# Moving eight 128x1024 integer additions from VectorE to GpSimd in a fused attention and rational-FFN kernel

## The chip, the cores and the metric

The kernel runs on one core of a Trainium2 chip. The metric is the device time of one execution in microseconds (us), from a run without a profile; lower is better. Three such runs of the kernel before gave 809.83, 808.62 and 809.86 us, with a median of 809.83. A profile is one further execution that is traced. Engines: PE is TensorE (matrix products), DVE is VectorE, ACT is ScalarE, POOL is GpSimd, SP is SyncE, whose queue issues the transfers between HBM and the on-chip memory.

## The reference

There are two parts. The first is a two-step attention for 8 batches and 8 heads with 576 tokens of 64 features: 32 packed queries `p` attend over `k` and `v`, and then the 576 queries `q` attend over the 32 packed rows. The second is a feed-forward layer on the 4608 tokens with 512 features, whose activation is a ratio of two polynomials.

```python
def sm_attn(qq, kk, vv):
    s = scale * np.matmul(qq, kk.transpose(0, 1, 3, 2))
    s = s - np.max(s, axis=-1, keepdims=True)
    a = np.exp(s)
    a = a / (np.sum(a, axis=-1, keepdims=True) + 1e-09)
    return np.matmul(a, vv)
p_packed = sm_attn(p, k, v)
out = sm_attn(q, p_packed, p_packed)
...
h = x @ w_in
h2 = h * h
h3 = h2 * h
P = a[0] + a[1] * h + a[2] * h2 + a[3] * h3
Q = 1.0 + np.abs(b[0]) * np.abs(h) + np.abs(b[1]) * h2
g = P / (Q + 1e-06)
return (g @ w_out).astype(np.float32)
```

The inputs come in as float64. `w_in` is 512x2048, `w_out` is 2048x512.

## The kernel before, in words

**Units.** The feed-forward work is cut into 128 units: 8 batches, two halves of 288 tokens, and 8 chunks `c` of 256 hidden features. For a unit, PE makes `h` from the attention weights (tiles `AH`, `AL`: a high and a low part of each number) and from a chunk matrix `m`; ACT and DVE make the ratio (`Y`, `U`, `V`), ACT and POOL split the result in a high and a low part (`gh`, `gl`), and PE multiplies these by the split `w_out` (tiles `w`) into `acc`. The chunk matrix `m` of a batch is made by `m_chunk` (L731): PE multiplies the batch's packed rows by chunk `c` of the converted `w_in` (tile `win`), and ACT splits the product. So the first eight units of the first batch need the chunks `c` = 0 to 7 of `win` one after the other, and nothing of `m` can be made for a chunk before its conversion is over. Later batches find `win` ready.

**Conversion of the float64 weights.** `convert` (L389) turns one pair of blocks of float64 words into float32. The raw words are loaded by SP into buffers that are free for the time being (`m0` to `m3` first, then buffers of the `w` ring). A pair of `w_in`'s words is one chunk `c`: 128x1024 numbers. Its steps are: ACT scales the high halves `hi` in place (L406) and brings the upper bits of the low halves `lo` into `di` (L408), which for `w_in` is the chunk's own place in `win`; DVE takes the sign (L409), shifts `hi` by three bits and puts the sign in (L410), and adds `di` to it as 32-bit integers (L411). In the trace and in the order this addition appears as `CUSTOM_DVE_ANT_0` or `ISA` with 128x2048 uint16. For `w_in` the sum is the finished chunk. For `w_out` it is split in two parts on ACT and POOL (L416). There are 8 such pairs of `w_in`, 7 pairs of `w_out`, and two single blocks of `w_out`.

**What sets the order.** All operations are recorded, not issued, and then put in order by `Planner` (L33): it gives each a cost by engine and columns, schedules them several times over the five engines by their dependences, and keeps the order of the best of its schedules. Each engine then runs its list strictly in order. So moving a recorded operation to another engine, at another cost, makes the planner work out a new order for every engine. The planner's costs know nothing of two engines that hold each other up. Because all operations are issued in one place, the profile gives them all the line L216, and groups have to be told apart by tiles.

**Names.** `kx` holds the keys, the queries and the scores of a batch's attention, `small` its maxima and sums, `pn` its packed queries, `nat` loaded blocks of `k`, `q`, `v`. For the first batch DVE subtracts the maxima and multiplies by the reciprocal sums in `kx` and makes `AL` (`eng` in L510); for the later ones POOL does. `G` collects the columns that the main products leave out. In the order's names the first number counts tiles: `m_1_82`, `m_2_83`, `m_3_115`, `m_4_116`, `w_3_117`, `w_4_118`, `w_6_120` and `w_8_132` are the raw words of the chunks 0 to 7 of `w_in`; `w_5_119` and `w_7_121` are the first raw pairs of `w_out`, and `w_11_158` is the first split pair.

Of the kernel before, what the change touches and what calls it, by code (L numbers as in the profile page):

```python
# [15 lines left out]
I32 = mybir.dt.int32  # L16
# [231 lines left out]
def attention_rational_ffn(  # L248
# [35 lines left out]
    nc = Planner(tc.nc)  # L284
# [75 lines left out]
    def load_words(n):  # L360
        while len(words_in) < min(len(words), converted + n):
            r = len(words_in)
            kind, i, n2 = words[r]
            used = [x for x, _ in words_in]
            free = [x for x, end in room if r < end and x not in used[converted:]]
            free = [x for x in free if x[0] is not w_ring or x[1] < NCH - 2 or started]
            if not free and r == converted and n2 == 1:
                free = [(o_ring, 0)]
            if not free:
                return  # L370
            x = min(free, key=lambda x: max((j for j in range(r) if used[j] == x), default=-1))
            raw = x[0].at(x[1], [P, n2 * 512], I64)
            if kind == "in":
                c = i // 2
                for y in range(2):
                    src = w_in[2 * y * P : (2 * y + 2) * P, c * CF : (c + 1) * CF].rearrange("(x p) f -> p x f", p=P)
                    nc.sync.dma_start(raw[:, 512 * y : 512 * (y + 1)].rearrange("p (x y) -> p x y", x=2), src)
            else:
                for y in range(n2):
                    nc.sync.dma_start(raw[:, 512 * y : 512 * (y + 1)], w_out[(i + y) * P : (i + y + 1) * P, :])  # L380
            words_in.append((x, raw))
# [3 lines left out]
    def split(x, hi, lo, eng=nc.gpsimd):  # L385
        nc.scalar.copy(hi, x)
        eng.tensor_sub(lo, x, hi.bitcast(F32))

    def convert():  # L389
        nonlocal converted  # L390
        if converted == len(words):
            return
        load_words(AHEAD)
        (kind, i, n), raw = words[converted], words_in[converted][1]
        x = 4 if kind == "in" else n
        w = raw.bitcast(I32).rearrange("p (x y two) -> p x y two", x=x, two=2)
        lo, hi = w[:, :, :, 0], w[:, :, :, 1]

        if kind == "in":
            dst = win[:, i // 2]  # L400
            di = dst.bitcast(I32)
        else:
            dst = lo.bitcast(F32)
            di = w_ring.at(i // 2, [P, n * DM], I32) if n == 2 else full_ring.next(dtype=I32)
            di = di.rearrange("p (x y) -> p x y", x=n)
        nc.scalar.activation(hi.bitcast(F32), hi.bitcast(F32), AF.Copy, scale=REBIAS)  # L406

        nc.scalar.activation(di, lo.bitcast(U32), AF.Copy, scale=2.0**-29)  # L408
        nc.vector.tensor_scalar(lo, hi, -0x80000000, None, ALU.bitwise_and)  # L409
        nc.vector.scalar_tensor_tensor(hi, hi, 3, lo, ALU.logical_shift_left, ALU.bitwise_or)  # L410
        nc.vector.tensor_add(dst.bitcast(I32), hi, di)  # L411
        if kind == "out":
            if i // 2 not in W:
                W[i // 2] = w_ring.at(i // 2)
            for y in range(n):
                split(dst[:, y, :], *(W[i // 2][:, (i + y) % 2, x, :] for x in range(2)))  # L416
        converted += 1
        load_words(AHEAD)
# [454 lines left out]
    for _ in range(PRE):  # L873
        convert()
# [30 lines left out]
    for u in range(NU + LAG + 2):  # L905
        if u < NU:
            pipe[u] = hidden(*units[u])
        stage(u)
        if 0 <= u - LAG < NU:
            acc_block(u - LAG, 0)  # L910
        filler(2 * u)
        stage(u)
        stage(u - 2)
        stage(u - 1)
        for x in rem.get(u, ()):
            remainder(*x)
        convert()
        while converted < len(words) and due(words[converted]) <= u + 1:
            convert()
        if 0 <= u - LAG < NU:  # L920
            acc_block(u - LAG, 1)
        filler(2 * u + 1)
# [30 lines left out]
```

## Time and profile before

| | |
|---|---|
| median of three runs | 809.83 us |
| the profiled execution | 808.45 us |
| its span, first to last instruction | 806.7 us |
| mean granted TensorE clock | 0.958 |
| busy PE, DVE, ACT, POOL | 745.5, 709.1, 666.0, 463.9 us |
| instructions on PE, DVE, ACT, POOL | 5416, 1310, 1482, 462 |

Of the profiled execution's 808.45 us, 1.75 lie outside the span. The page cuts the span in 40 slices of 20.2 us; a view by stages gives each engine's busy time in stretches that one chooses; a view by groups gives the count, the busy time and the mean of all instructions of one shape; a timeline lists the instructions of an engine with their start and duration. In a timeline an instruction's duration overlaps the next one's start by a little, so that the place that it takes in its engine's time is the distance between two starts.

### The profile page before, as it was taken

How to read it: one execution, taken by the hardware profiler on the slowest of the kernel's cores; microseconds unless marked ns; L12 is line 12 of the kernel's file. 1: busy time of each engine (PE TensorE's matmuls, PEld its weight loads, DVE VectorE, ACT ScalarE, POOL GpSimd, SP SyncE). 2: the span in 40 equal slices, each digit the busy share in tenths (PEclk: the TensorE clock that was granted, in tenths of full speed). 3: DMA queues.
4: the chain of work that ended last, by engine and by line, in shares of the span. 5: the costliest groups of instructions: out<-in, count | busy, mean ns of one | idle time of the engine just before them, and what ended most of it. 6: DMA issues, size and time to landing. Idle time of an engine off the chain costs nothing.

```text
span 806.7 us, 15198 instructions
## 1 busy us (share of the span) xinstructions
PE 745.5 (92%) x5416; PEld 585.4 (73%) x5416; DVE 709.1 (88%) x1310; ACT 666.0 (83%) x1482; POOL 463.9 (58%) x462
## 2 busy tenths in 40 slices
PE   6376686899999999999999999999999999999997
PEld 4154464578877788768878788678877887778886
DVE  2988999898899788998899789998899789998873
ACT  4788797799888798889888798889888788998972
POOL 0003564675568455766578555756568456766663
PEclk9765799799999999999999999999999999999999
DMA  8993238202550206220730209120820214000001
GB/s 267 280 298 110 105 78 110 43 5 79 67 86 1 79 18 96 56 57 28 94 58 1 82 15 119 33 56 27 103 49 5 75 33 67 1 2 27 27 1 39
DMA packets 168876, 56.04 MB, mean 69 GB/s; under 512 B 140384, under 2 KB 158048, under 8 KB 168800
## 3 DMA queue, kind: packets, MB, share of 16 engines
q1 hardware_dynamic: 168800, 55.07, 31.4%
q8 instruction: 42, 0.69, 0.4%
q14 instruction: 34, 0.28, 0.1%
HBM read 45.62 MB, written 9.44 MB: 68 GB/s over the span
## 4 chain that ended last, share of the span: by engine, by line
PE 70%; DVE 10%; ACT 8%; SPq 4%; DMA 4%; issue 2%; POOL 1%; DVEq 0%; POOLq 0%
PE acc L216 35%; PE h L216 22%; PE at L216 13%; DVE Y L216 5%; SPq L216 4%; ACT Y L216 2%; DVE w L216 1%; ACT U L216 1%; ACT V L216 1%; ACT w L216 1%; DMA w<-in_q_dram 1%; ACT sq L216 1%; DVE V L216 1%; POOL w L216 1%; DVE kx L216 1%
## 5 line engine op out<-in xcount | busy, mean ns | idle before, releaser
L216 PE MATMUL acc<-w,gh 128*128 128x512 f32 x1024 | 330.5, 405 | 19.3 <-ACT w L216 15.0
L216 PEld LDWEIGHTS acc<-w,gh 128*128 128x128 f32 x1024 | 186.7, 191 | 72.7 <-ACT w L216 16.6
L216 POOL TENSOR_TENSOR U<-U,sq 128x576 f32<-128x576 f32 x118 | 168.9, 1432 | 75.4 <-ACT U L216 43.3
L216 PE MATMUL h<-AH,m 128*128 128x288 f32 x1024 | 192.0, 309 | 8.8 <-DVE Y L216 6.1
L216 POOL TENSOR_TENSOR gl<-Y,gh 128x512 fp32r<-128x512 f32 x128 | 167.7, 1310 | 50.5 <-ACT gh L216 23.3
L216 PE MATMUL acc<-w,gl 128*128 128x512 f32 x512 | 193.2, 398 | 0.3 <-POOL gl L216 0.3
L216 PEld LDWEIGHTS h<-AH,m 128*128 128x128 f32 x1024 | 162.7, 195 | 40.5 <-DVE Y L216 23.1
L216 ACT ACTIVATE Y<-h,abS 128x288 f32<-128x288 f32 x256 | 125.2, 509 | 23.5 <-PE h L216 19.3
L216 DVE TENSOR_TENSOR Y<-Y,h 128x288 f32<-128x288 f32 x256 | 109.9, 446 | 32.0 <-ACT Y L216 12.0
L216 ACT ACTIVATE sq<-h 128x288 f32<-128x288 f32 x236 | 97.5, 416 | 40.2 <-PE h L216 34.1
L216 DVE SCALAR_TENSOR_TENSOR Y<-Y,abS,h 128x288 f32<-128x288 f32 x256 | 125.5, 508 | 2.2
L216 DVE SCALAR_TENSOR_TENSOR Y<-Y,abS,V 128x576 f32<-128x576 f32 x128 | 103.4, 808 | 22.7 <-ACT V L216 22.0
L216 PEld LDWEIGHTS acc<-w,gl 128*128 128x128 f32 x512 | 96.8, 189 | 28.0 <-issue 8.5
L216 PE MATMUL h<-AL,m 128*128 128x288 f32 x512 | 113.0, 302 | 0.0
L216 POOL COPY G<-Y 128x64 f32<-128x64 f32 x128 | 35.5, 277 | 125.8 <-DVE Y L216 109.1
L216 ACT ACTIVATE U<-h 128x288 f32<-128x288 f32 x256 | 98.1, 421 | 8.7 <-PE h L216 4.3
L216 ACT ACTIVATE V<-U,one 128x576 f32<-128x576 f32 x128 | 98.0, 766 | 5.8 <-DVE Y L216 5.6
L216 DVE SCALAR_TENSOR_TENSOR Y<-V,Y 128x576 f32<-128x576 f32 x128 | 95.8, 749 | 1.8
L216 DVE SCALAR_TENSOR_TENSOR V<-U,V 128x576 f32<-128x576 f32 x128 | 96.4, 753 | 0.0
L216 ACT CAST gh<-Y 128x512 fp32r<-128x512 f32 x128 | 81.2, 634 | 7.4 <-DVE Y L216 7.0
L216 PEld LDWEIGHTS h<-AL,m 128*128 128x128 f32 x512 | 85.1, 194 | 0.9 <-issue 0.8
L216 ACT ACTIVATE V<-V 128x576 f32<-128x576 f32 x128 | 84.6, 661 | 0.6
(123 smaller groups left out, 813.2 us busy)
## 6 DMA issues: line engine op xcount, KB each, us to landing
nat<-in_k_dram SPq DMA_DIRECT2D x56, 144.0 KB, 4.1
nat<-in_q_dram SPq DMA_DIRECT2D x56, 144.0 KB, 4.2
out_dram<-o SPq DMA_DIRECT2D x15, 512.0 KB, 2.9
w<-in_moe_w_out_dram SPq DMA_DIRECT2D x14, 512.0 KB, 5.0
nat<-in_v_dram SPq DMA_DIRECT2D x28, 256.0 KB, 3.6
m<-in_moe_w_in_dram SPq DMA_DIRECT2D x8, 512.0 KB, 9.6
w<-in_moe_w_in_dram SPq DMA_DIRECT2D x8, 512.0 KB, 5.5
nat<-in_k_dram SPq DMA_DIRECT2D x2, 512.0 KB, 4.8
```

What stands on the lines that cost most here:

```text
L216: getattr(getattr(self.nc, engine), name)(*args, **kwargs)
```

## The change

The addition of `convert` goes to POOL when the words are those of `w_in`, and stays on DVE for those of `w_out`:

```diff
         nc.vector.scalar_tensor_tensor(hi, hi, 3, lo, ALU.logical_shift_left, ALU.bitwise_or)
-        nc.vector.tensor_add(dst.bitcast(I32), hi, di)
+
+        eng = nc.gpsimd if kind == "in" else nc.vector
+        eng.tensor_add(dst.bitcast(I32), hi, di)
         if kind == "out":
```

The planner makes a new order from this. The lists of all engines differ up to about a third of the kernel; DVE's is the same again from its row 432 of 1302 on, which is in the fifth half-batch.

On DVE, at the conversion of the chunks 1 and 2 in the first attention, this stood before (`ISA` is the addition):

```order
L216 SCALAR_TENSOR_TENSOR m_2_83<-m_2_83 128x1024
L216 TENSOR_REDUCE small<-kx_1_84 128x18
L216 TENSOR_TENSOR kx_1_84<-kx_1_84,small 128x576
L216 TENSOR_SCALAR small<-small 128x18
L216 ISA win<-m_2_83,win 128x2048
L216 RECIPROCAL small<-small 128x18
L216 STREAM_TRANSPOSE kx_1_84<-kx_1_84 128x576
L216 TENSOR_TENSOR kx_1_84<-kx_1_84,small 128x576
L216 SCALAR_TENSOR_TENSOR m_3_115<-m_3_115 128x1024
L216 STREAM_TRANSPOSE kx_1_84<-kx_1_84 128x576
L216 TENSOR_TENSOR AL_1_86<-kx_1_84,AH_1_85 128x576
```

and this stands there now:

```order
L216 SCALAR_TENSOR_TENSOR m_2_83<-m_2_83 128x1024
L216 TENSOR_REDUCE small<-kx_1_84 128x18
L216 TENSOR_TENSOR kx_1_84<-kx_1_84,small 128x576
L216 TENSOR_SCALAR small<-small 128x18
L216 TENSOR_SCALAR m_3_115<-m_3_115 128x1024
L216 RECIPROCAL small<-small 128x18
L216 RECIPROCAL root<-root 128x1
L216 SCALAR_TENSOR_TENSOR m_3_115<-m_3_115 128x1024
L216 TENSOR_REDUCE small<-kx_1_84 128x18
L216 TENSOR_TENSOR kx_1_84<-kx_1_84,small 128x576
L216 TENSOR_SCALAR small<-small 128x18
L216 TENSOR_SCALAR m_4_116<-m_4_116 128x1024
```

The additions are gone from the list, and the shifts of the next chunks (`SCALAR_TENSOR_TENSOR m`) stand earlier. That of chunk 1 stood behind the subtraction of the maxima in both halves of the scores and now stands ahead of the second of these (the first `TENSOR_TENSOR kx` of the rows now); that of chunk 2 stood behind both multiplications by the reciprocal sums and now stands ahead of them (the second `TENSOR_TENSOR kx` of the rows now is the first of them).

On POOL, from the packed queries of the second batch (`pn_2_107`) to the second split pair of `w_out` (`w_14_174`), this stood before:

```order
L216 COPY pn_2_107<-pn_2_107 128x2x64
L216 COPY G<-Y_2_127 128x2x32
L216 TENSOR_TENSOR gl_1_156<-Y_2_127,gh_1_155 128x512
L216 COPY pn_3_243<-pn_3_243 128x2x64
L216 TENSOR_TENSOR w_11_158<-w_5_119,w_11_158 128x512 x2
L216 COPY G<-Y_3_138 128x2x32
L216 TENSOR_TENSOR gl_2_171<-Y_3_138,gh_2_170 128x512
L216 TENSOR_TENSOR w_14_174<-w_7_121,w_14_174 128x512 x2
```

and this stands there now:

```order
L216 TENSOR_TENSOR win<-w_3_117,win 128x1024
L216 TENSOR_TENSOR win<-w_4_118,win 128x1024
L216 COPY pn_2_107<-pn_2_107 128x2x64
L216 COPY G<-Y_2_127 128x2x32
L216 TENSOR_TENSOR gl_1_156<-Y_2_127,gh_1_155 128x512
L216 COPY G<-Y_3_138 128x2x32
L216 TENSOR_TENSOR gl_2_171<-Y_3_138,gh_2_170 128x512
L216 TENSOR_TENSOR w_11_158<-w_5_119,w_11_158 128x512
L216 TENSOR_TENSOR win<-w_6_120,win 128x1024
L216 TENSOR_TENSOR w_11_158<-w_5_119,w_11_158 128x512
L216 COPY G<-Y_4_151 128x2x32
L216 COPY pn_3_243<-pn_3_243 128x2x64
```

The additions of the chunks 0 to 5 stand ahead of all other work of POOL behind its first copy; that of chunk 6 stands between the two halves of the first split pair of `w_out`, and that of chunk 7 (not shown) stands behind the second split pair.

On SP the loads of the raw words `w_3_117` now stand ahead of the four loads of `nat_3_104` instead of behind them, those of `pn_2_107` ahead of `w_6_120`, and those of `nat_6_153` behind `w_12_172` and `w_15_175`, which go into the buffers of the raw words `w_6_120` and `w_7_121`.

## The prediction

> **What bounds the kernel now.** I read the page first, for the engines' busy time over the whole and by slices.
>
> ```profile
> span 806.7 us, 15198 instructions
> PE 745.5 (92%) x5416; PEld 585.4 (73%) x5416; DVE 709.1 (88%) x1310; ACT 666.0 (83%) x1482; POOL 463.9 (58%) x462
> PE   6376686899999999999999999999999999999997
> DVE  2988999898899788998899789998899789998873
> ```
>
> PE is the busiest, but in its first eight slices of 20.2 us it is far from full, and DVE is nearly full there. The view by stages shows the change from one regime to the other (busy us of each engine, then the granted TensorE clock):
>
> ```profile
> 25.00:50.00 25.00, 11.82 (x84) 6.31 (x85) 23.59 (x40) 18.27 (x32) 0.00 (x0) 0.58 0.95 232
> 50.00:75.00 25.00, 15.48 (x110) 11.32 (x108) 21.79 (x33) 23.45 (x44) 5.73 (x6) 0.64 0.66 214
> 75.00:100.00 25.00, 18.88 (x119) 13.89 (x120) 23.28 (x36) 18.42 (x39) 13.39 (x9) 0.70 0.32 118
> 100.00:125.00 25.00, 21.73 (x175) 15.50 (x174) 24.93 (x42) 22.26 (x44) 15.15 (x13) 0.98 0.51 85
> 125.00:150.00 25.00, 16.73 (x104) 10.73 (x104) 24.88 (x45) 17.56 (x36) 15.49 (x15) 0.77 0.56 80
> 150.00:780.00 630.00, 623.48 (x4519) 498.84 (x4512) 568.29 (x1066) 541.13 (x1239) 401.73 (x403) 1.00 0.25 47
> ```
>
> From 150 us on PE is busy 623.48 of 630 us (99%): it is the bound, and no saving on DVE counts there. From 25 to 150 us DVE is busy 118.47 of 125 us (95%), and ACT leads only from 50 to 75 us (23.45 of 25). All conversions lie in this ramp. So a microsecond that the ramp gains or loses on DVE is about a microsecond at the end: the order of all engines comes back to what it was in the fifth half-batch, and PE runs through the rest.
>
> **The change part by part.** *What DVE gets rid of.* In the groups that keep shapes apart, eight additions for `w_in`, four with raw words in `m` and four in `w`, take about 1.22 us each; below them are the nearest rows of POOL.
>
> ```profile
> L216 DVE CUSTOM_DVE_ANT_0 win<-m,win 128x2048 uint16<-128x2048 uint16 x4 | 4.9, 1226 | 0.0
> L216 DVE CUSTOM_DVE_ANT_0 win<-w,win 128x2048 uint16<-128x2048 uint16 x4 | 4.9, 1216 | 0.0
> L216 POOL TENSOR_TENSOR U<-U,sq 128x576 f32<-128x576 f32 x118 | 168.9, 1432 | 75.4 <-ACT U L216 43.3 <-ACT sq L216 15.8 <-DVE Y L216 9.2
> L216 POOL TENSOR_TENSOR gl<-Y,gh 128x512 fp32r<-128x512 f32 x128 | 167.7, 1310 | 50.5 <-ACT gh L216 23.3 <-issue 15.4 <-POOL G L216 6.9
> ```
>
> The timeline of DVE in the first attention shows the place that an addition takes:
>
> ```profile
> 24.05 1.23 DVE L216 CUSTOM_DVE_ANT_0 win<-m,win 128x2048 uint16<-128x2048 uint16 x1
> 25.20 0.84 DVE L216 STREAM_TRANSPOSE kx<-at 128x288 f32<-128x288 f32 x2
> 27.34 0.72 DVE L216 TENSOR_TENSOR kx<-kx,small 128x576 f32<-128x576 f32 x1
> ...
> 31.42 1.17 DVE L216 SCALAR_TENSOR_TENSOR m<-m 128x1024 int32<-128x1024 int32 x1
> 32.49 0.75 DVE L216 TENSOR_REDUCE small<-kx 128x18 f32<-128x576 f32 x1
> 33.15 0.76 DVE L216 TENSOR_TENSOR kx<-kx,small 128x576 f32<-128x576 f32 x1
> 33.89 1.23 DVE L216 CUSTOM_DVE_ANT_0 win<-m,win 128x2048 uint16<-128x2048 uint16 x1
> 35.03 0.27 DVE L216 RECIPROCAL small<-small 128x18 f32<-128x18 f32 x1
> ...
> 37.61 0.78 DVE L216 STREAM_TRANSPOSE kx<-kx 128x576 f32<-128x576 f32 x1
> 38.30 0.73 DVE L216 TENSOR_TENSOR AL<-kx,AH 128x576 fp32r<-128x576 f32 x1
> ...
> 42.47 1.45 DVE L216 STREAM_TRANSPOSE kx<-nat 128x576 f32<-128x576 f32 x2
> 45.33 0.45 DVE L216 TENSOR_TENSOR Y<-Y,h 128x288 f32<-128x288 f32 x1 [1.41 <-ACT U L216]
> ```
>
> From 33.89 to the next start at 35.03 are 1.14 us; eight such places are 9.1 us.
>
> *What POOL gets.* No row shows an integer addition on POOL. The two rows above differ by 122 ns for 64 columns, 1.91 ns a column; 512 columns beyond the 512 make 1310 + 977 = 2287 ns. That is my estimate, 2.29 us. Bounds: half of 1310 for the low end, if integers went far faster (0.7 us), and twice 2.29 for the high end (4.6 us), if they had a slower path. I take 2.29, since it continues two rows of the same form. POOL is idle from 25 to 50 us and has 5.73 busy of 25 behind that, so its time costs nothing by itself: 8 x 2.29 = 18.3 us fit.
>
> *What DVE gets back.* The timelines of POOL and DVE show that certain instructions of the two exclude each other:
>
> ```profile
> 76.58 1.28 POOL L216 TENSOR_TENSOR gl<-Y,gh 128x512 fp32r<-128x512 f32 x1 [0.16 <-ACT gh L216]
> ...
> 87.17 3.02 POOL L216 COPY G<-Y 128x64 f32<-128x64 f32 x1
> ...
> 112.33 1.61 POOL L216 TENSOR_TENSOR gl<-Y,gh 128x512 fp32r<-128x512 f32 x1 [2.74 <-ACT gh L216]
> ```
>
> ```profile
> 77.00 1.41 DVE L216 TENSOR_SCALAR w<-w 128x1024 int32<-128x1024 int32 x1
> ...
> 87.14 0.69 DVE L216 TENSOR_SCALAR w<-w 128x1024 int32<-128x1024 int32 x1
> 87.74 2.36 DVE L216 SCALAR_TENSOR_TENSOR w<-w 128x1024 int32<-128x1024 int32 x2
> ...
> 113.43 1.60 DVE L216 SCALAR_TENSOR_TENSOR w<-w 128x1024 int32<-128x1024 int32 x1
> ```
>
> The sign operation at 77.00 took 1.41 us where the same at 87.14 took 0.69; it ended at 78.41, 0.55 after POOL's subtraction ended at 77.86. The shift at 113.43, which reads two tensors in the on-chip memory, took 1.60 instead of the 1.17 of its sister at 31.42; it ended 1.09 after POOL did at 113.94. And the copy at 87.17, a small one, took 3.02 and ended at 90.19, when two shifts of DVE had ended at 90.10. So while POOL makes an addition of 2.29 us, DVE cannot run an operation with two such inputs, nor the sign operation. The attention's `TENSOR_TENSOR kx` and `AL` have two such inputs; in before they ran while POOL was idle, so no row shows them held, and I give them what the row at 113.43 shows.
>
> Now I go down DVE's new order behind each shift that releases an addition, taking 0.1 us for the release. Chunk 0: three transposes, a maximum and a transpose come next, which nothing holds; they take 27.34 - 25.20 = 2.14, so the subtraction behind them is held 2.39 - 2.14 = 0.25. Chunk 1: a sum (33.15 - 32.49 = 0.66), then a subtraction, held 1.7. Chunk 2: the same with a multiplication, 1.7. Chunk 3: a transpose (0.69 from 37.61 to 38.30), then `AL`, held 1.7. Chunks 4 and 5: two transposes of `nat`, then operations that read `h` from the matrix products' memory, 0. Chunk 6: between 0 and 1.4, as it depends on where ACT lets the addition start; I take 0.7. Chunk 7 comes in a run of sign operations, shifts and additions of `w_out`, between 0 and 1.6: if POOL gets in first, DVE is held 1.6; if DVE's next operation always goes ahead, as in the row at 87.17, POOL waits instead and DVE loses nothing. I take 0.8. The sum is 0.25 + 3 x 1.7 + 0.7 + 0.8 = 6.85 us; its bounds are 0, if the attention's operations are not held, and about 16, if an addition takes 4.6 us (2.3 more at each of the chunks 0 to 3).
>
> On chunk 7 the Trainium skill differs from the row: by "SBUF — State Buffer", section "SBUF: two separate sides", the one of the two engines that starts first has the shared port pair for its whole instruction and the other blocks, so a waiting POOL instruction should come in between two of DVE's. The copy at 87.17 was passed over by the second shift. By the page's rule the hold for chunk 7 would be 1.6 and the sum below -1.5 us; by the row it would be 0 and the sum -3.1.
>
> *The sum.* DVE: -9.1 + 6.85 = -2.25, in round numbers -2.2 us.
>
> *What else moves.* The new order lets SP load the words of chunk 4 ahead of four blocks of `k`, and `v`'s second half behind two pairs of `w_out`.
>
> ```profile
> 19.40 10.78 SPq L216 DMA_DIRECT2D nat<-in_k_dram  x4
> 30.22 2.21 SPq L216 DMA_DIRECT2D w<-in_moe_w_in_dram  x4
> ...
> 73.17 32.11 SPq L216 DMA_DIRECT2D w<-in_moe_w_out_dram  x8
> ```
>
> ```profile
> 73.68 2.56 POOL L216 TENSOR_TENSOR w<-w,w 128x512 fp32r<-128x512 f32 x2 [2.19 <-ACT w L216]
> ```
>
> The blocks of `k` are issued half of 2.21 later, to about 31.3 us, and are first read at 42.47: covered. The pair of `w_out` at 73.17 goes into the buffer of chunk 6's raw words. It waited for DVE's addition and now waits for POOL's, which stands behind the first half of `w_11`'s split: 73.68 + 1.28 + 2.29 = 77.25, 4 us later. This pair's sign operation comes at 87.14, 14 us after its issue, so I price the delay at nothing; were the cover gone, it would cost up to about 1 us of DVE. Behind the sixth addition on POOL stand `G`, `gl` and the splits; POOL's idle time covers them. The small root computation moves to gaps: nothing.
>
> So the profiled execution's 808.45 would become 806.2, and the median of 809.83 becomes **807.6 us**. A measurement of this kernel can tell about 0.2% (1.6 us) from no change. With holds between 4 and 9 us this case gives -5 to 0 us: 804.8 to 809.8.
>
> **The rivals.** *The holds are small (full gain).* If DVE's attention operations run beside POOL, or POOL's integers are quick, DVE saves its 9.1 us. The stretch from 50 to 75 us, where ACT leads, has three of the eight additions and would keep about half of their 3.4 us, so 9.1 - 1.7 = 7.4: 802.4 us. For it speaks that no row shows a float operation of the attention held; against it, the row at 113.43.
>
> *The first attention comes late and nothing makes it up (slower).* The place is the first operation of the first unit, at 45.33, before which DVE had been idle for 1.41 us. Up to there DVE loses three additions (3.4 us), but gets holds of 0.25 + 5.1 and, by the new order, chunk 4's sign operation and shift (0.7 + 1.1) that came behind it: +3.7 on its former end at 43.92, 47.6 instead of 45.33, so 2.3 us late. In the main case DVE gets this back, because it has chunk 4's work done and no addition for the chunks 3 to 5. But from 50 to 75 us ACT is busy 94%, and its own work then starts late. If ACT stays behind until PE is the bound, the end is 2.3 us later: 812.1 us; with additions of 4.6 us the four holds would make it 9 more, which I hold for unlikely and leave out of the range. It decides when ACT reaches unit 1 more than 2 us later than now. The skill's "GPSIMD Engine Reference", section "4.1 Engine selection", would have the two-input addition left on VectorE, since GpSimd takes about twice as long; 2.29 against 1.22 us agrees with that.
>
> *Nothing changes.* ACT paces the ramp to 100 us, so that DVE's saving becomes idle time: 809.8 us. Against it stands DVE's 24.93 and 24.88 of 25 us from 100 to 150.
>
> That the change doesn't do what it says is excluded: the new lists show the eight additions on POOL.
>
> **How the numbers follow.** My forecast has 0.45 (0.33 of it beyond 1.6 us), the full gain 0.15, the slower case 0.28, no change 0.12. Faster by over 0.2%: 0.33 + 0.15 = 0.48. Within: 0.12 + 0.12 = 0.24. Slower: 0.28. The range reaches below to the full gain, and above to the slower case with somewhat longer additions: 802.0 to 813.5. Beyond its ends I leave about half of the full gain's chance below and a third of the slower one's above, 0.17.
>
> **What would show each step.** In the changed kernel's profile: the group `win` on POOL with a mean near 2.29 us; `TENSOR_TENSOR kx` and `AL` of the first attention with 2.4 instead of 0.73 us, three of them; DVE busy from 25 to 150 us less by 2 to 3 us or the same work done earlier, and the first `Y<-Y,h` near 47.6. I am wrong if these operations keep 0.73 us (then the gain is larger), if the additions take over 3 us, or if the ramp's length moves for a reason in the new order that I priced at nothing.

## The result and the profile after

The kernel with the change takes 805.23 us (median of six runs, 803.53 to 808.72), the kernel before 809.70 (six runs, 808.62 to 810.05). The ratio is 0.9947, with a 95% interval of 0.9927 to 0.9967: faster by 4.5 us, where 2.2 were forecast. The profiled execution took 803.53 us. Its page begins so (span, busy time of the engines, and the first slices of 20 us):

```profile
span 801.8 us, 15225 instructions
PE 738.4 (92%) x5416; PEld 580.3 (72%) x5416; DVE 710.1 (89%) x1302; ACT 665.6 (83%) x1482; POOL 480.1 (60%) x470
PE   6465695999999999999999999999999999999997
DVE  2999999998899789998899789998899789998883
```

Eight instructions have left DVE (1310 to 1302) and come to POOL (462 to 470). But DVE is not less busy: 710.1 us, and 709.1 before. The view by stages, with the columns of before, says where:

```profile
25.00:50.00 25.00, 11.82 (x92) 6.79 (x93) 24.69 (x34) 17.03 (x31) 9.77 (x5) 0.59 1.02 266
50.00:75.00 25.00, 15.51 (x88) 11.42 (x87) 24.05 (x38) 23.95 (x48) 13.91 (x10) 0.66 0.49 154
75.00:100.00 25.00, 16.54 (x149) 11.24 (x149) 25.00 (x34) 22.84 (x46) 15.93 (x12) 0.80 0.40 136
100.00:125.00 25.00, 20.12 (x173) 16.42 (x172) 25.00 (x43) 20.51 (x40) 12.84 (x12) 0.93 0.60 93
125.00:150.00 25.00, 18.41 (x113) 12.82 (x119) 23.95 (x43) 18.42 (x40) 12.68 (x14) 0.86 0.48 92
150.00:780.00 630.00, 623.96 (x4525) 497.73 (x4524) 569.66 (x1069) 540.91 (x1239) 403.23 (x404) 1.00 0.25 46
```

From 25 to 150 us DVE is busy 122.69 us in place of 118.47: the ramp is fuller. From 150 us on PE is busy 623.96 of 630 us, as before. ACT, which had 18.42 us of work from 75 to 100 us, has 22.84. The gain is made in this ramp: PE's busy time over the whole less that up to 150 us leaves 641.2 us of work behind 150 us, and 645.6 before. The groups that the prediction named, first on POOL, then on DVE (count, busy us and mean ns behind the bar):

```profile
L216 POOL TENSOR_TENSOR win<-w,win 128x1024 int32<-128x1024 int32 x4 | 10.0, 2511 | 9.2 <-DVE w L216 5.6 <-ACT U L216 3.7
L216 POOL TENSOR_TENSOR win<-m,win 128x1024 int32<-128x1024 int32 x4 | 9.6, 2412 | 26.7 <-DVE m L216 20.6 <-ACT m L216 3.3 <-DMA nat<-in_k_dram 2.8
```

```profile
L216 DVE TENSOR_TENSOR kx<-kx,small 128x576 f32<-128x576 f32 x4 | 6.6, 1648 | 0.0
L216 DVE TENSOR_TENSOR AL<-kx,AH 128x576 fp32r<-128x576 f32 x2 | 3.3, 1649 | 0.0
```

An addition takes 2.41 us on POOL (2.51 with one that had to wait). The means of 1648 and 1649 ns mix held and unheld operations, as the timelines of POOL and DVE show for the first attention:

```profile
22.72 2.41 POOL L216 TENSOR_TENSOR win<-m,win 128x1024 int32<-128x1024 int32 x1 [16.63 <-DVE m L216]
28.46 2.41 POOL L216 TENSOR_TENSOR win<-m,win 128x1024 int32<-128x1024 int32 x1 [3.33 <-ACT m L216]
```

```profile
25.21 0.72 DVE L216 TENSOR_TENSOR kx<-kx,small 128x576 f32<-128x576 f32 x1
...
28.91 2.59 DVE L216 TENSOR_TENSOR kx<-kx,small 128x576 f32<-128x576 f32 x1
...
34.08 2.58 DVE L216 TENSOR_TENSOR kx<-kx,small 128x576 f32<-128x576 f32 x1
...
40.53 2.55 DVE L216 TENSOR_TENSOR AL<-kx,AH 128x576 fp32r<-128x576 f32 x1
43.01 0.68 DVE L216 TENSOR_SCALAR w<-w 128x1024 int32<-128x1024 int32 x1
...
44.28 1.21 DVE L216 SCALAR_TENSOR_TENSOR w<-w 128x1024 int32<-128x1024 int32 x1
45.41 1.43 DVE L216 STREAM_TRANSPOSE kx<-nat 128x576 f32<-128x576 f32 x2
47.15 0.45 DVE L216 TENSOR_TENSOR Y<-Y,h 128x288 f32<-128x288 f32 x1 [0.31 <-ACT U L216]
```

Three operations are held, 2.55 to 2.59 us each instead of 0.72; the first of them ends at 31.50, 0.63 behind POOL's addition (28.46 + 2.41 = 30.87). The first unit starts at 47.15 instead of 45.33. All that is nearly what was forecast. What was not forecast stands at the end of the last row: DVE had waited 1.41 us for ACT's `U` there and now waits 0.31. The view of waits of DVE from 40 to 160 us (us in total, times, longest) has this in one row for before and one for after:

```profile
DVE Y L216 <- ACT U L216: 5.2, 5, 1.7
```

```profile
DVE Y L216 <- ACT U L216: 0.6, 2, 0.3
```

These waits have shrunk by 4.6 us, and the kernel by 4.5. That the two sizes agree does not yet make the one the cause of the other; the table behind the experiments sets them side by side for every kernel.

### The profile page after: what moved, and what is told of

Read it like the earlier page. It is cut to its first block, busy times and chain, and to the rows that moved or that the text cites. A ratio compares the mean times of both kernels' runs of the same rounds, so it can differ in the third digit from the quotient of the medians.

```text
span 801.8 us, 15225 instructions
## 1 busy us (share of the span) xinstructions
PE 738.4 (92%) x5416; PEld 580.3 (72%) x5416; DVE 710.1 (89%) x1302; ACT 665.6 (83%) x1482; POOL 480.1 (60%) x470
## 4 chain that ended last, share of the span: by engine, by line
PE 72%; DVE 13%; ACT 8%; DMA 3%; issue 2%; SPq 2%; POOL 0%; DVEq 0%; ACTq 0%
PE acc L216 36%; PE h L216 23%; PE at L216 13%; DVE Y L216 5%; DVE w L216 3%; SPq L216 2%; ACT Y L216 2%; ACT U L216 1%; ACT V L216 1%; DMA m<-in_moe_w_in_dram 1%; ACT sq L216 1%; DVE o L216 1%; DMA w<-in_moe_w_out_dram 1%; DMA rv<-in_v_dram 1%; DVE U L216 1%
## 5 line engine op out<-in xcount | busy, mean ns | idle before, releaser
L216 PE MATMUL h<-AH,m 128*128 128x288 f32 x1024 | 189.7, 307 | 16.0 <-DVE Y L216 12.6
L216 PEld LDWEIGHTS h<-AH,m 128*128 128x128 f32 x1024 | 160.6, 193 | 46.2 <-DVE Y L216 29.6
L216 POOL COPY G<-Y 128x64 f32<-128x64 f32 x128 | 33.7, 263 | 111.4 <-DVE Y L216 102.3
```

Of the source, the lines that this page charges most:

```text
L216: getattr(getattr(self.nc, engine), name)(*args, **kwargs)
```

## Experiments

There were two theories at first. By the forecast's, the additions that left DVE are the gain and the holds the price. By the rival, the planner's new order is the gain, and where the additions run does not matter. Each experiment was timed beside the kernel before, on the same chip, 5 to 12 times; its ratio compares the two. The chips differ between groups of experiments, so that medians of different experiments are not compared with each other to a microsecond.

**The new order, with the additions on DVE.** The planner sees the additions on POOL, and they are issued on DVE (the edit is against the changed kernel).

```diff
-            engine, calls = self.ops[i]
+            engine, calls = self.moved.get(i, self.ops[i][0]), self.ops[i][1]
...
         eng = nc.gpsimd if kind == "in" else nc.vector
         eng.tensor_add(dst.bitcast(I32), hi, di)
+        nc.moved.update({len(nc.ops) - 1: "vector"} if kind == "in" else {})
```

> The planner is told what the changed kernel tells it, so every engine's list is that of the changed kernel, but the eight additions are issued on VectorE, each at the place of the plan. First theory (the engine made the gain: 9.1 us off VectorE less about 7 of holds): without the moved additions most of the 4.5 us goes away; the new order without the move is worth about what is left over, 4.5 - 2.2 = 2.3 us, so about 807.4 us. Rival (the new order made the gain, and the engine nothing, since VectorE is as long busy as before): about 805.2 us, as the changed kernel. Second rival (an order made for GpSimd is bad with VectorE's additions in it): about 810 us or more.

Measured: 804.63 us, ratio 0.9938 (0.9925 to 0.9951). The whole gain is there with no addition moved. DVE's waits for `U` are all but gone as well:

```profile
DVE Y L216 <- ACT V L216: 1.8, 2, 1.0
DVE Y L216 <- ACT U L216: 0.4, 1, 0.4
```

The first unit starts even later than in the changed kernel:

```profile
48.34 0.77 DVE L216 STREAM_TRANSPOSE kx<-nat 128x576 f32<-128x576 f32 x1
49.03 0.42 DVE L216 TENSOR_TENSOR Y<-Y,h 128x288 f32<-128x288 f32 x1
```

It starts at 49.03, 3.7 us behind before's 45.33, with no wait in front of it, since conversion work stands where DVE used to wait. A late first unit is not a loss by itself.

**The old order, with the additions on POOL.** The reverse: planned as before, issued on GpSimd. The line in `issue` is the same as above.

```diff
         nc.vector.tensor_add(dst.bitcast(I32), hi, di)
+        nc.moved.update({len(nc.ops) - 1: "gpsimd"} if kind == "in" else {})
```

> The converse: the planner plans as before, and the eight additions go to GpSimd without a change of any other list. First theory (engine): about 2.2 us less than before, 807.5 us, with holds of about 1.7 us at the operations behind each shift that read two tensors. Rival (order): as before, 809.7 us, or slower, since GpSimd's additions take 2.4 us and hold VectorE.

Measured: 808.86 us, ratio 0.9993 (0.9981 to 1.0004). Moving the additions alone gives nothing that can be told from no change. Its waits of DVE show where the saving goes:

```profile
DVE Y L216 <- ACT U L216: 7.5, 6, 3.1
DVE w L216 <- ACT w L216: 1.2, 1, 1.2
DVE Y L216 <- ACT V L216: 0.6, 2, 0.4
```

DVE's wait for `U` grows from 5.2 to 7.5 us. Up to the end of the eleventh unit DVE is busy 127.2 us in place of 129.5, less by 2.3, and idle 26.6 us in place of 22.2: what the move saves, holds deducted, turns into waiting, and more than that. This unit ends 2.1 us later (153.8 us for 151.7), in a profiled execution that is 1.1 us longer than before's (809.59 us for 808.45).

**Shorter holds.** In the changed kernel each addition is cut in four pieces of 256 columns, so that DVE can come in between them.

```diff
-            for name, args, kwargs in calls:
+            for name, args, kwargs in self.cut(calls) if i in self.moved else calls:
...
+    def cut(self, calls):
+        (name, args, kwargs), = calls
+        return [(name, [x[:, j : j + 1] for x in args], kwargs) for j in range(4)]
```

> The changed kernel with the same lists, but each addition on GpSimd is issued as four of 256 columns. If a waiting VectorE operation gets in between two pieces, the first attention's held operations take at most 0.73 + 0.7 us instead of 2.59. First theory (the holds give back most of the saving, each microsecond of them is one at the end): about 3 us faster than the changed kernel, 802 us. Rival (VectorE's holds in the first attention are not what the end waits for, as ACT and the transfers pace it there): within 1 us of the changed kernel. Second rival (the pieces' fixed costs make the additions longer and a chunk later): slower than the changed kernel by 1 us or more.

Measured: 804.01 us, ratio 0.9932 (0.9918 to 0.9945). The first attention on DVE:

```profile
29.68 0.92 DVE L216 TENSOR_TENSOR kx<-kx,small 128x576 f32<-128x576 f32 x1
30.52 0.71 DVE L216 TENSOR_SCALAR small<-small 128x18 f32<-128x18 f32 x1
...
34.09 1.33 DVE L216 TENSOR_TENSOR kx<-kx,small 128x576 f32<-128x576 f32 x1
...
40.32 0.87 DVE L216 TENSOR_TENSOR AL<-kx,AH 128x576 fp32r<-128x576 f32 x1
...
46.53 0.41 DVE L216 TENSOR_TENSOR Y<-Y,h 128x288 f32<-128x288 f32 x1
```

The operations that were held 1.85 us each now lose 0.21, 0.62 and 0.14, but others lose some instead: the small `TENSOR_SCALAR` takes 0.71 us where it took 0.17 (at 31.42 in the changed kernel). Summed over all of DVE's operations from 22 us to the first unit, each against its free duration, 4.6 us are lost here and 5.6 in the changed kernel: the pieces spread the holds rather than remove them, the first unit starts only 0.62 us earlier, and the interval of the ratio overlaps that of the change. So this run cannot say what the holds are worth.

**Another order of the same work.** All is as in the kernel before, but the planner prices an addition of 1024 columns on DVE at 200 ns more.

```diff
-        return fixed + per * self.columns(aps[1] if name.startswith("reduce") else aps[0])
+        return fixed + per * self.columns(aps[1] if name.startswith("reduce") else aps[0]) + 200 * (name == "tensor_add" and engine == "vector" and self.columns(aps[0]) == 1024)
```

> The kernel before with all work on its old engines; only the planner's price of the eight additions on VectorE is 200 ns higher, which gives another order up to the fifth half-batch and the same behind it. Theory that the order by itself moves the time by several microseconds (the gain of the change is one such draw): a difference from before of 1.5 to 5 us, either way. Theory that orders of the same work are alike: within 1 us of 809.7.

Measured: 806.61 us, ratio 0.9962 (0.9949 to 0.9975). An order that has nothing to do with the change takes 3 us off as well, and here DVE waits 4.4 us for `U` in three waits.

**Which part of the new order.** For the next four kernels the program works out both orders and joins them; every addition stays on DVE. In the first, only SP's list of transfers is the new one; in the others all engines follow the new order for what it plans before 34, 58 or 90 us, and behind that the old one. (These are the planner's own times. On DVE its last step ahead of 58 us is chunk 6's shift, which starts at 66.78 us in the trace of that kernel, and its last step ahead of 90 us stands near 105 us of the trace.)

```diff
+        at = lambda i: (new if self.ops[i][0] == "sync" else old)[i]
```

```diff
+        first = sorted((i for i in range(len(new)) if new[i] < 34000), key=lambda i: (new[i], i))
+        done = set(first)
+        return first + sorted((i for i in range(len(old)) if i not in done), key=lambda i: (old[i], i))
```

> All eight additions on VectorE. Only SP's list of loads is the new one (the words of chunk 4 ahead of four blocks of k, the second half of v behind two pairs of w_out); the lists of the four compute engines are those of before. Theory that earlier loads make the gain: about 804.6 us, as with all lists new. Rival (the order of the compute engines makes it): 809.4 us within 1 us, or slower, if a load that comes later is missed.

Measured: 813.07 us, ratio 1.0046 (1.0033 to 1.0059), slower by 3.7 us. DVE's timeline shows where it starts:

```profile
17.65 0.16 DVE L216 SCALAR_TENSOR_TENSOR root<-ab 128x1 f32<-128x1 f32 x1 [3.83 <-DMA ab<-in_moe_b_dram]
```

The new list brings the coefficients `ab` later. In DVE's old list the small root computation stands early and waits 3.83 us for them, and the first unit then starts at 48.37 us, 3.0 later than before; the new order also puts the root's steps later, so that there is no such wait. Half of an order can be worse than either order.

> All eight additions on VectorE. The operations that the new plan puts ahead of the first product h stand first, in the new order (the first attention and the conversions of the chunks 0 to 2); all others follow in the order of before. Theory that the earlier shifts of the chunks 1 to 3 in the first attention make the gain: most of 4.8 us, so 805 to 806 us. Rival (the gain is made between the first unit and the last chunk, where ACT is busy 94% from 50 to 75 us): within 1 us of 809.4.

Measured: 809.14 us, ratio 1.0003 (0.9993 to 1.0013): no change. The first attention's new order, with the old order behind it, is not the gain.

> As the run before it, but the new order holds up to the conversion of chunk 5 and the first product of unit 3. Theory of the first attention: no better than the run before it. Theory of the stage where ACT leads: about half of the gain, 806 to 808 us.

Measured: 812.48 us, ratio 1.0035 (1.0022 to 1.0047), slower. The joint seems to cost here: DVE's two longest waits are 3.54 us for `U` at 85.77 and 2.05 for `V` at 77.54, behind the place where the lists change over.

> As the run before it, but the new order holds up to the conversion of the last chunk (7) and the products of unit 6. If the gain is made up to there, 804.6 us within 1 us; if a part of it comes from the order of what follows (the remaining words of w_out and the second attention), about 806 to 807 us.

Measured: 803.66 us, ratio 0.9924 (0.9910 to 0.9939): the whole gain, again with no addition moved. So what the new order does up to the planner's 90 us is enough, and what it does up to 58, with the old order behind it, is not. DVE's waits from 40 to 160 us:

```profile
DVE Y L216 <- ACT Y L216: 1.7, 2, 1.5
DVE Y L216 <- ACT V L216: 1.1, 2, 0.7
DVE Y L216 <- ACT U L216: 0.4, 1, 0.4
```

**One thing at a time.** In the kernel before, the stage from 60 to 85 us seemed to have three faults. DVE converted `w_out`'s first pair in turns with chunk 6; PE waited 4.91 us for this pair's copies, with the next units' `h` behind them in its list; ACT made conversions for later pairs ahead of these copies. These are the rows of PE and DVE before, and PE's waits for ACT's copies of `w` from 60 to 100 us:

```profile
73.65 1.22 PE L216 MATMUL acc<-w,gh 128*128 128x512 f32 x2 [4.91 <-ACT w L216]
69.87 1.47 DVE L216 CUSTOM_DVE_ANT_0 w<-w,w 128x2048 uint16<-128x2048 uint16 x1
PE acc L216 <- ACT w L216: 7.6, 2, 4.9
```

Each was changed alone in the old order, and then all three together. `put` gives a step (by its number) another time in the planner's old schedule, in ns, and with it another place in its engine's list.

```diff
+        put = {408: 63500.0, 409: 63600.0}
+        at = lambda i: put.get(i, old[i])
```

Steps 408 and 409 are chunk 6's sign operation and shift; the pair's addition stands at 62983.

> All eight additions stay on VectorE and the old order stays, but for one thing: on VectorE the first two steps of chunk 6's words of w_in (the shift and the combination that writes w) go behind the addition of w_out's first pair. In the kernel before, TensorE stands still for 4.91 us at 73.65 until ScalarE's copies of that pair come. Theory A (lockstep on VectorE: the pair that TensorE waits for is late because another pair is converted in the middle of it): the addition ends about 1.9 us earlier, TensorE's wait shrinks to about 3 us, and the kernel takes about 806 to 807 us. Theory B (ScalarE's list sets it: it is busy without a gap from 59.8 to 77.6 with conversions for later pairs, and the copies stand behind them): the addition comes earlier and the copies do not, 809 us. Rival C (the gain has no single place, and needs the whole new order of this stage): 809 us.

Measured: 810.62 us, ratio 1.0002 (0.9990 to 1.0014). The addition did not come earlier at all (69.87 before):

```profile
69.57 0.81 DVE L216 SCALAR_TENSOR_TENSOR Y<-Y,abS,V 128x576 f32<-128x576 f32 x1 [1.96 <-ACT V L216]
70.30 1.22 DVE L216 CUSTOM_DVE_ANT_0 w<-w,w 128x2048 uint16<-128x2048 uint16 x1
...
84.77 3.48 DVE L216 TENSOR_SCALAR w<-w 128x1024 int32<-128x1024 int32 x2
```

A step of the running unit stands ahead of it and waits 1.96 us for ACT's `V`: chunk 6's steps had only filled this wait. Theory A does not hold: with chunk 6 out of its way the pair is no earlier. Later two sign operations take 3.48 us where two took 1.35 before (at 65.51); POOL was making the second pair's split from 84.68 to 87.69.

The next kernel puts `h` of the two units that follow ahead of each group of `acc` products on PE.

```diff
+        put = {i: old[j] - 1 for j, k in ((377, 437), (377, 461), (448, 512), (448, 529)) for i in range(k, k + 6)}
```

> All eight additions stay on VectorE and the old order stays, but for one thing: on TensorE the products h of the two units that follow go ahead of the first and of the second group of acc products, which wait for the copies of w_out's pairs. Theory D (the list of TensorE sets it: h stands behind products that wait, and ScalarE and VectorE then wait for h, 2.31 and 0.74 us on ScalarE at 79.94 and 81.17): those two waits go, VectorE's wait for them with it, and the kernel takes 805 to 807 us. Theory B or C: h could go no earlier anyway, because the buffers or VectorE's next steps are not ready, 809 us, or slower, since now the acc products stand behind h.

Measured: 811.00 us, ratio 1.0019 (1.0007 to 1.0031), slower, by less than the bound of 0.2%. PE's timeline:

```profile
76.11 1.33 PE L216 MATMUL h<-AH,m 128*128 128x288 f32 x4 [7.70 <-DVE Y L216]
...
79.15 1.48 PE L216 MATMUL acc<-w,gh 128*128 128x512 f32 x3
```

`h` cannot go ahead: it waits 7.70 us, to 76.11, for DVE to finish with the last unit's `h`, and now the `acc` products wait behind it. Theory D does not hold: in this kernel PE waits for DVE at `h`.

The third moves three conversions on ACT (one of chunk 7's, both of the third pair's of `w_out`) behind the copies and the `U` of the running unit.

```diff
+        put = {482: 65900.0, 488: 65910.0, 489: 65920.0}
```

> All eight additions stay on VectorE and the old order stays, but for one thing: on ScalarE three conversions of later pairs (the second half of chunk 8's words of w_in and both of the third w_out pair's, 1.24, 1.30 and 1.32 us) go behind the copies of w_out's first pair and the U of the running unit. Theory B: the copies start at about 71.3, when VectorE's addition ends, in place of 72.76, and U of the running unit comes at about 72.5 in place of 73.86; VectorE's next Y, which waits for it at 74.57, comes over 1 us earlier: 806 to 808 us. Theories A and D: 808.5 to 809.5. Rival C: 809 us.

Measured: 808.25 us, ratio 0.9980 (0.9967 to 0.9993), about 1.6 us faster. The waits of DVE and of PE (60 to 100 us) follow:

```profile
DVE Y L216 <- ACT U L216: 4.0, 5, 1.4
```

```profile
PE acc L216 <- ACT w L216: 6.9, 3, 3.7
```

The wait for `U` falls from 5.2 to 4.0 us and PE's longest wait for the copies from 4.91 to 3.7. By this ACT's list is a part of it (theory B), with about a third of the gain; but the gain is only about the 0.2% that can be told from no change, and two other kernels here, at 3.6 us of waits for `U`, gain nothing.

> All eight additions stay on VectorE and the old order stays, but for the three changes of the other runs together: on VectorE the first pair of w_out is finished before chunk 6 is begun, on TensorE the products h go ahead of acc products that wait, on ScalarE the conversions for later pairs go behind the copies and the U that are wanted first. If what these lists do at 60 to 85 us is what the new order gains, this comes to 804 to 806 us, the mean busy time of ScalarE in 75 to 100 us rises from 18.4 to over 20 us, and TensorE's wait of 4.91 us shrinks to under 3. If the gain is spread over the whole order of the stage (rival C), 808 to 810 us.

Measured: 810.07 us, ratio 1.0008 (0.9996 to 1.0019): no change, and ACT has 19.39 us of work from 75 to 100 us, not the over 20 expected. The three do not add up; moving `h` ahead makes PE wait for DVE again, here 9.1 us at its longest. Of the theories, rival C (the gain needs the new order of this stage as a whole) is the one that these runs do not speak against; no run tests it by itself.

All kernels in one table, with DVE's waits for `U` in 40 to 160 us of the profiled execution. The ratio compares each kernel with the kernel before on the same chip; the medians come from several chips and don't rank the kernels exactly:

| kernel | median us | ratio to before | waits for `U`, us (times) |
|---|---|---|---|
| before | 809.70 | 1 | 5.2 (5) |
| after | 805.23 | 0.9947 | 0.6 (2) |
| new order, additions on DVE | 804.63 | 0.9938 | 0.4 (1) |
| new order, additions in four on POOL | 804.01 | 0.9932 | 0.8 (1) |
| new order to chunk 7 | 803.66 | 0.9924 | 0.4 (1) |
| another order | 806.61 | 0.9962 | 4.4 (3) |
| ACT's later pairs last | 808.25 | 0.9980 | 4.0 (5) |
| old order, additions on POOL | 808.86 | 0.9993 | 7.5 (6) |
| new to the first unit | 809.14 | 1.0003 | 3.6 (5) |
| pair first on DVE | 810.62 | 1.0002 | 3.6 (4) |
| three together | 810.07 | 1.0008 | 4.3 (5) |
| `h` first on PE | 811.00 | 1.0019 | 6.5 (5) |
| new to chunk 5 | 812.48 | 1.0035 | 3.9 (2) |
| only the loads new | 813.07 | 1.0046 | 4.7 (6) |

The four kernels of about 804 to 805 us are those with under 1 us of waits for `U`, and no other has under 3.6. Within the others the column does not order the times, since other waits and holds come in. That this goes together is shown; that these waits are what the time hangs on is not. PE's waits from 60 to 100 us for ACT's copies of `w` go with it too: 2.0 to 2.4 us in the four, and 5.1 to 8.2 in the others but for the two with `h` first, where PE waits 11.4 and 12.6 us for DVE instead. And DVE's waits of all kinds from 40 to 160 us do not go with it: they are 7.2 us with the additions in four, of which 4.3 is one wait for ACT's `w`, and 4.0 us in "new to the first unit". Which of the new order's moves up to the planner's 90 us makes the gain stays open. The kernel with the new order to chunk 7 has the lowest median, but its interval (0.9910 to 0.9939) overlaps that of the change (0.9927 to 0.9967), so it is not shown to beat it.

## Why the prediction was right in its sign and wrong in its reason

**The additions on POOL**: forecast 2.29 us, measured 2.41. The two float rows of the same form gave a good price for integers.

**The holds**: forecast 0.25 + 3 x 1.7 + 0.7 + 0.8 = 6.85 us. Measured: 0 for chunk 0 (the row at 25.21), 1.87, 1.86 and 1.83 for the three of the attention, none for chunks 4 and 5, none for chunk 6, and 1.54 for chunk 7. The sum is 7.1 us. For chunk 7 the rows of POOL and DVE are these:

```profile
83.73 2.80 POOL L216 TENSOR_TENSOR win<-w,win 128x1024 int32<-128x1024 int32 x1 [2.43 <-DVE w L216]
```

```profile
83.57 0.69 DVE L216 TENSOR_SCALAR w<-w 128x1024 int32<-128x1024 int32 x1
84.17 0.76 DVE L216 STREAM_TRANSPOSE kx<-nat 128x576 f32<-128x576 f32 x1
84.87 2.75 DVE L216 SCALAR_TENSOR_TENSOR w<-w 128x1024 int32<-128x1024 int32 x1
```

POOL first waits for the sign operation, gets in beside the transpose, and the shift then takes 2.75 us instead of 1.21. That agrees with the rule of the Trainium skill's "SBUF — State Buffer", section "SBUF: two separate sides" (whichever of the two starts first has the port pair for its whole instruction). It does not settle what the prediction weighed against that rule: a transpose stood between DVE's two operations here, and the copy at 87.17 was passed over where two shifts stood next to each other. That a waiting instruction of POOL would come in between two such operations was the prediction's own inference, and this row doesn't test it.

**DVE's net gain**: forecast 2.2 us; with the old order DVE was busy 2.3 us less up to the eleventh unit. The size was right.

**The step that failed**: "a microsecond that the ramp gains or loses on DVE is about a microsecond at the end". DVE is busy 95% of the ramp, but 6.4 of the remaining 6.5 us are waits for ACT (5.2 for `U`, 1.2 for `w`), and with the old order DVE's saving went into such waiting: 0.9993. This is the rival "nothing changes", at 0.12; for the move alone it spoke of the right mechanism, and the 24.9 of 25 us from 100 to 150 us that spoke against it are only what comes behind the waits.

**What else moves**: priced at nothing, and worth all of it: 5.0 us with the new order alone (0.9938). The prediction saw that the planner re-orders every engine, costed the few rows that it could trace to one operation, and took the rest for neutral. It isn't: the new orders and part-orders tried here lie between 803.66 and 813.07 us.

**The slower rival** (first unit late): its place was right, 47.15 for 47.6, but the delay costs nothing: with the additions on DVE the first unit starts at 49.03 and the kernel is no slower. Conversion work was done in time that DVE had waited, and ACT has 22.48 us of work from 75 to 100 us in that kernel, where before it had 18.42. **The full gain** (802.4) spoke of holds that cost nothing, and no run here was without them while the additions were on POOL, so that it wasn't tried; but the new order with the additions on DVE has no such holds, does 9.1 us more of additions, and takes 804.63 us.

The size came out 2.4 us off because one term, the move, gave nothing where 2.2 were expected, and the other, the order, gave 5 where nothing was expected. That the time came out faster, as forecast, and near the forecast is luck: it did so for another reason than the one given.

## What to carry to other kernels

Where a planner sets the order, test a change in two halves, the new order with the old engine and the old order with the new engine, before a gain is put down to what was moved. An engine that is busy 95% need not be what bounds the time, if the rest of its time is waiting for another: read which wait ends last, unit by unit, and whether the saved work only makes that wait longer. A fault that is plain in the trace need not be worth anything when mended alone: of three mended here one gave nothing, one cost about 1.5 us, one gained about 1.6, and together they gave nothing.

## What was not expected of the hardware

An integer addition of 128x1024 on POOL takes 2.41 us, and in four pieces 2.85 us when nothing is in its way, so that a further start costs about 0.15 us (an estimate: a third of the difference). With DVE coming in between, eight pieces took 8.71 us, 1.09 each:

```profile
23.11 2.85 POOL L216 TENSOR_TENSOR win<-m,win 128x256 int32<-128x256 int32 x4 [17.08 <-DMA m<-in_moe_w_in_dram]
29.23 8.71 POOL L216 TENSOR_TENSOR win<-m,win 128x256 int32<-128x256 int32 x8 [3.28 <-ACT m L216]
```

These times fit two engines that come in by turns. The holds of the three operations that were held before are 0.14 to 0.62 us in place of 1.85, but ten operations are held in the first attention in place of three.

DVE's `Y<-Y,abS,V` and `V<-U,V`, whose `V` lies in the matrix products' memory, ran beside chunk 6's addition (POOL, 70.14 to 72.57) at 0.80 us (at 70.58) and 0.75 us (at 71.73), the means of their groups over the whole kernel being 804 and 750 ns: not held, like those that read `h`.
